# Half-channel loads of k and v, and TensorE and VectorE trading channel chunks, in a long-convolution and MLP kernel

## The chip, the cores and the metric

The kernel runs on one core of one Trainium2 chip. The metric is the device time of one execution in microseconds (us); lower is better. Every comparison uses runs of the fast state, and each kernel was timed beside runs of the kernel before on the same chip.

## The reference, cut to what matters

```python
def _A_ref(q, k, v, shift_k, ssm_k, ssm_D):          # 1 x 2048 positions x 512 channels, bf16
    k_shift = sum(k_pad[:, t:t + S, :] * shift_k[:, ks - 1 - t] for t in range(4))   # 4 taps per channel
    kv = k_shift * v
    # y = causal convolution of kv with the 2048 taps of ssm_k, by FFT of length 4096
    y = irfft(rfft(kv_pad) * rfft(kf_pad))[:S] + kv * ssm_D
    return q * y

def _B_ref(x, w1, b1, w2, b2):                        # 512 -> 1376 -> 512
    return gelu(_layernorm(x) @ w1 + b1) @ w2 + b2

x = A_q; x = x + A; x = x + B; x = x + A; x = x + B   # A is the same both times, but for its q
```

## The kernel before: the parts that matter

The kernel lists its operations, and a list scheduler with tuned priorities puts each on an engine's queue. An engine takes its queue in that order. The FFT is two stages of matmuls with tables. The 512 channels are four chunks of 128. Two chunks get their 4 taps from VectorE as elementwise operations; the other two from TensorE, which transposes k and multiplies by diagonal matrices of taps.

```python
PE_CH, PO_CH = (0, 1), ()                  # chunks of TensorE; the rest are VectorE's
LOADS = ("k", "v", 0, 1, 2, 3, 4, 5, 6, 7) # order of the transfers; 0..7 are pieces of the table S2
...
for b in range(4):                         # the long filter ssm_k, 4 blocks of 128 channels
    dma(A(0, 128, R_HRAW + b * 2048, [1, 2048]), dr(A_ssm_k, ...), 1 << 19)
...
dma(A(0, 128, R_SR, [1, 2048]), dr(A_shift_k, 0, [0, 128], [1, 2048]), 1 << 19)   # taps, 128-fold
...                                        # k: 16 positions x 512 channels in each partition
    for j in range(4):                     # a piece has 4 KB in a row
        dma(A(0, 128, R_K + 1536 + 2048 * j, [1, 2048]), dr(A_k, 2048 * j, ...), 1 << 19)
...                                        # filter: 16 transposes of 128 columns, 32 bytes apart (L740)
        src = [A(0, 128, R_HRAW + b * 2048 + a, [16, 128]) for a in range(16)]
            for a in range(16):
                r = e.transpose(QB(tl, 0, 128, a * 128, [1, 128]), src[a], IDN)
        evac(BOTH, ...)                    # PSUM to SBUF on ScalarE (L665) or VectorE (L666)
        o = A(0, 1, R_HP + b * 2048, [64, 32], [1, 4])
        tt(o, o, A(0, 1, R_D + 128 * b, ...), ALU.add, 200.0, POOL)   # adds D to the filter: 128 elements
def stage1(...):  ...   # 16 matmuls of 64 columns for a PSUM tile (L757), then an evacuation
def stage2(...):  ...   # 8 matmuls with the table S2 for a tile (L770), then an evacuation
def shift_pe(i):  ...   # 16 transposes of k (L801), 32 matmuls by tap diagonals (L813), product with v (L820)
def shift_tt(i):  ...   # 7 VectorE operations of 128x2048 for a chunk: tensor_tensor, both inputs in SBUF
```

## Time and profile before

| | before |
|---|---|
| median of 3 runs | 245.31 us (244.29 to 245.67) |
| span of the profiled run | 242.7 us |
| TensorE, VectorE, ScalarE, GpSimd busy | 229.0, 176.1, 144.7, 32.8 us |
| filter transposes (L740) | 4.80 to 10.66 us |
| VectorE's first operation on k | 17.75 us |
| first matmul of the MLP (L1045) | 86.86 us |

The first 87 us are the convolution. From 87 us on, the MLP's matmuls fill TensorE for 155.7 us. So the change has to be judged by when that first MLP matmul starts. The prediction shows the lines of this profile.

### The profile page before, as it was taken

What the parts mean: (1) busy time and instruction counts of PE and PEld (TensorE: products, weight loads), DVE (VectorE), ACT (ScalarE), POOL (GpSimd) and SP (SyncE); (2) the same over time, 40 slices, a digit from 0 to 9 for tenths busy, and PEclk for the clock granted to TensorE, in tenths of its full rate; (3) what the DMA queues carried; (4) which work ended last, traced back from release to release, by engine and by line L of the source; (5) the groups of instructions that cost most, each with busy time, mean ns of one, the idle gap of its engine ahead of it and who ended that gap; (6) DMA issues with size and microseconds to landing.
All of it is one profiled execution on the core that took longest, in us unless ns stands there. A gap on an engine that the chain in (4) does not pass through costs nothing.

```text
span 242.7 us, 5658 instructions
## 1 busy us (share of the span) xinstructions
PE 229.0 (94%) x2399; PEld 155.7 (64%) x2399; DVE 176.1 (73%) x359; ACT 144.7 (60%) x224; POOL 32.8 (14%) x71
## 2 busy tenths in 40 slices
PE   7959999786899999999999999999999999999995
PEld 3859989665899877777667665655444444444543
DVE  0459999999999998899999998797734760313022
ACT  2987899989998976755355444387004584005600
POOL 2330000000004121232131113003101010000000
PEclk9997999999999999999999999999999999999999
DMA  6999959999991000421120203302230111412012
GB/s 236 361 407 406 407 107 206 194 195 241 398 376 47 0 3 0 45 44 23 24 45 0 46 2 64 68 0 45 45 71 18 43 43 22 68 43 86 0 57 76
DMA packets 32938, 27.68 MB, mean 114 GB/s; under 512 B 17585, under 2 KB 28176, under 8 KB 32784
## 3 DMA queue, kind: packets, MB, share of 16 engines
q1 hardware_dynamic: 32766, 27.21, 40.8%
q8 instruction: 19, 0.31, 0.5%
q10 hardware_dynamic: 146, 0.10, 0.2%
q14 instruction: 7, 0.06, 0.1%
HBM read 17.34 MB, written 2.10 MB: 80 GB/s over the span
## 4 chain that ended last, share of the span: by engine, by line
PE 69%; DVE 18%; DMA 5%; ACT 3%; SPq 2%; issue 1%; POOL 1%; DVEq 0%
PE ps L1045 32%; PE ps L1078 30%; DVE ar L660 11%; DMA ar<-in_A_k_dram 5%; DVE ar L666 4%; ACT ar L665 3%; PE ps L813 2%; SPq L649 2%; PE ps L757 2%; DVE sm L970 1%; PE ps L1067 1%; DVE ar L820 1%; PE ps L801 1%; DVE ar L985 1%; POOL sm L978 1%
## 5 line engine op out<-in xcount | busy, mean ns | idle before, releaser
L1050 ACT ACTIVATE ar<-ps,sm 128x256 bf16<-128x256 f32 (+5 forms) x143 | 68.0, 521 | 73.2 <-PE ps L1045 37.9
L1045 PE MATMUL ps<-ar 128*128 128x256 bf16 (+4 forms) x572 | 82.1, 297 | 0.0
L665 ACT ACTIVATE ar<-ps 128x1024 bf16<-128x1024 f32 (+2 forms) x78 | 74.3, 1059 | 10.0 <-PE ps L757 3.8
L1078 PE MATMUL ps<-ar 128*128 128x512 bf16 (+1 forms) x341 | 79.2, 379 | 0.0
L1045 PEld LDWEIGHTS ps<-ar 128*128 128x128 bf16 (+1 forms) x572 | 53.1, 100 | 28.8 <-ACT ar L665 0.4
L660 DVE TENSOR_TENSOR ar<-ar 128x512 bf16<-128x512 bf16 (+2 forms) x104 | 63.2, 645 | 3.1 <-DMA ar<-in_A_k_dram 2.4
L1078 PEld LDWEIGHTS ps<-ar 128*128 128x128 bf16 (+1 forms) x341 | 33.2, 98 | 35.1
L1082 DVE TENSOR_TENSOR ar<-ar,ps 128x512 bf16<-128x512 bf16 x31 | 20.8, 680 | 43.7 <-PE ps L1078 43.7
L970 DVE BATCH_NORM_STATS2 sm<-ar 128x6 f32<-128x512 bf16 (+1 forms) x68 | 42.9, 649 | 0.4
L985 DVE TENSOR_SCALAR ar<-ar,sm 128x512 bf16<-128x512 bf16 x64 | 23.5, 403 | 6.3 <-POOL sm L978 6.2
L757 PE MATMUL ps<-ar 128*64 128x128 bf16 x512 | 18.9, 231 | 3.0 <-issue 1.1
L978 POOL TENSOR_TENSOR sm<-sm 128x2 f32<-128x2 f32 (+2 forms) x26 | 20.2, 778 | 2.2
L757 PEld LDWEIGHTS ps<-ar 128*64 128x64 bf16 x512 | 16.3, 117 | 5.0 <-ACT ar L665 1.9
L666 DVE CAST ar<-ps 128x1024 bf16<-128x1024 f32 (+1 forms) x17 | 19.2, 1151 | 0.3 <-PE ps L770 0.2
L976 POOL TENSOR_SCALAR sm<-sm 128x2 f32<-128x2 f32 (+2 forms) x26 | 5.3, 205 | 101.7 <-DVE sm L972 101.4
L882 PE MATMUL ps<-ar 128*128 128x128 bf16 x256 | 15.1, 220 | 1.2 <-DVE ar L660 0.7
L882 PEld LDWEIGHTS ps<-ar 128*128 128x128 bf16 x256 | 14.6, 114 | 1.6 <-DVE ar L660 0.8
L858 PE MATMUL ps<-ar 128*128 128x64 bf16 x256 | 9.2, 193 | 2.8 <-ACT ar L665 2.3
L666 DVE COPY ar<-ps 128x2048 bf16<-128x2048 bf16 (+1 forms) x5 | 4.5, 904 | 9.6 <-PE ps L740 9.5
L972 DVE BATCH_NORM_AGGREGATE sm<-sm 128x2 f32<-128x6 f32 (+1 forms) x64 | 10.2, 173 | 0.5
L858 PEld LDWEIGHTS ps<-ar 128*128 128x128 bf16 x256 | 8.1, 98 | 3.8 <-ACT ar L665 2.9
L770 PE MATMUL ps<-ar 128*128 128x128 bf16 x128 | 8.2, 220 | 0.5 <-ACT ar L665 0.5
(30 smaller groups left out, 76.9 us busy)
## 6 DMA issues: line engine op xcount, KB each, us to landing
ar<-tab_s SPq DMA_DIRECT2D x8, 512.0 KB, 15.9
ar<-ar SPq DMA_DIRECT2D x16, 256.0 KB, 6.9
ar<-in_A_ssm_k_dram SPq DMA_DIRECT2D x4, 512.0 KB, 5.5
ar<-in_A_k_dram SPq DMA_DIRECT2D x4, 512.0 KB, 10.3
ar<-in_A_v_dram SPq DMA_DIRECT2D x4, 512.0 KB, 13.8
ar<-in_A_q_dram SPq DMA_DIRECT2D x4, 512.0 KB, 13.4
out_dram<-ar SPq DMA_DIRECT2D x7, 256.0 KB, 2.0
ar<-in_B_w_dram SPq DMA_DIRECT2D x1, 1376.0 KB, 12.0
```

What stands on the lines that cost most here:

```text
L660: return P.op(eng, lambda e: e.tensor_tensor(o, a, b, op), dur, reads=[a, b] + list(more), writes=[o])
L665: return e.activation(dst, src(), AF.Copy)
L666: return e.tensor_copy(dst, src())
L757: r = e.matmul(Q(tl, 64 * ri, 64, i * 128, [1, 128]), w, m, start=True, stop=True)
L882: r = e.matmul(Q(tl, 0, 128, i * 128, [1, 128]), w, m, start=q == 0, stop=q == 1)
L970: P.op(DVE, lambda e, sj=sj, x=x: e.bn_stats(sj, x), 40.0 + 1.1 * w, reads=[x], writes=[sj], gate=gate)
L978: P.op(POOL, lambda e: e.tensor_tensor(r, v, hf, ALU.pow), 430.0 + 150.0 * n, reads=[v, hf], writes=[r])
L985: P.op(DVE, lambda e: e.tensor_scalar(o, x, m, r, ALU.subtract, ALU.mult), 335.0, reads=[x, m, r], writes=[o])
L1045: r = e.matmul(Q(tl, 0, rows, 0, [1, w]), a, m, start=dk == 0, stop=dk == 3)
L1050: P.op(ACT, lambda e, dst=dst, tl=tl, rows=rows, bias=bias, w=w: e.activation(dst, Q(tl, 0, rows, 0, [1, w]), AF.Gelu_apprx_tanh, bias=bia ...
L1078: r = e.matmul(Q(tl, 0, 128, 0, [1, 512]), ins[fc][0], ins[fc][1], start=fc == 0, stop=fc == 10)
L1082: P.op(DVE, lambda e, x=x, tl=tl: e.tensor_tensor(x, x, Q(tl, 0, 128, 0, [1, 512]), ALU.add), 640.0, reads=[x], writes=[x], tile=tl)
```

## The change: intent and diff

The intent: VectorE waits for k, so let its chunks come first and alone. Each load of k and v takes half of the channels, so a row is 256 elements or 512 bytes. VectorE gets chunks 0 and 1, which lie in the first half, and TensorE gets chunks 2 and 3. The 128-fold tap transfer is replaced by a small one and two matmuls, the filter is loaded and transposed in halves, and all priorities are tuned anew.

```diff
-PE_CH, PO_CH = (0, 1), ()
-LOADS = ("k", "v", 0, 1, 2, 3, 4, 5, 6, 7)
+PE_CH, PO_CH = (2, 3), ()
+LOADS = ("k0", "k1", "v0", "v1") + tuple(range(16))
...
-        dma(A(0, 128, R_HRAW + b * 2048, [1, 2048]), ...)
+        for c in (0, 1024):
+            dma(A(0, 128, R_HRAW + b * 2048 + c, [1, 1024]), ...)
-    dma(A(0, 128, R_SR, [1, 2048]), dr(A_shift_k, 0, [0, 128], [1, 2048]), 1 << 19)
+    dma(A(0, 1, R_SR, [1, 2048]), dr(A_shift_k, 0, [0, 1], [1, 2048]), 4096, eng=ACT)
...
-            for j in range(4):
-                dma(A(0, 128, R_K + 1536 + 2048 * j, [1, 2048]), ...)
+            for a in (0, 8):      # half of the channels, 8 rows of 512 bytes in each partition
+                dma(A(0, 128, o + 512 * a + c, [512, 8], [1, 256]), ...)
...
-        tt(o, a, A(0, 128, R_SR + 512 * c, [1, 4], [4, 128]), ALU.mult, 1200.0, POOL)
+        # two matmuls by ones spread the taps; 8 GpSimd operations of 128x128 make the diagonals
...
-        src = [A(0, 128, R_HRAW + b * 2048 + a, [16, 128]) for a in range(16)]
+        for p in (0, 64):
+            src = [A(0, 128, R_HRAW + b * 2048 + a + 16 * p, [16, 64]) for a in range(16)]
...
-                r = e.transpose(QB(tl, 0, 128, a * 128, [1, 128]), src[a], IDN)
+                    r = e.transpose(QB(tl, p, 64, a * 128, [1, 128]), src[a], IDN)
...
-        tt(o, o, A(0, 1, R_D + 128 * b, [4, 32], [1, 4]), ALU.add, 200.0, POOL)
+        tt(o, o, A(0, 1, R_D + 128 * b, [4, 32], [1, 4]), ALU.add, {DVE: 130.0, POOL: 450.0}, (DVE, POOL))
```

The tables of priorities are cut. By line, the filter's transposes are L740 before and L754 after, stage 1 is L757 and L771, stage 2 is L770 and L784, the transposes of k are L801 and L815, their diagonal matmuls L813 and L827, the product with v L820 and L834, and the MLP's first matmul L1045 and L1059. In experiments these shift by a few lines.

## The prediction

> **What bounds the kernel now.** I first read the chain that ended last, then a table of stretches, then the timelines of VectorE and ScalarE around the stretch that the change touches, then the DMA view.
>
> The chain (start, length, what) begins with transfers:
>
> ```profile
> 5.91 11.82 DMA ar<-in_A_k_dram
> 17.82 1.15 PE ps L801 x16
> 18.98 3.83 PE ps L757 x40
> ...
> 86.86 1.90 PE ps L1045 x32
> ```
>
> Up to 17.73 us the end is set by the arrival of k. To 28.6 us the chain runs over TensorE, to 86 us over VectorE with some ScalarE, and from 86.9 us to the end over the matmuls of the MLP. The stretches say the same (length, then busy us of each engine, TensorE clock, DMA share, GB/s):
>
> ```profile
> 0.00:9.00 9.00, 7.24 (x60) 4.46 (x62) 0.02 (x1) 4.20 (x3) 2.23 (x10) 1.00 0.75 291
> 9.00:15.30 6.30, 5.79 (x166) 5.29 (x164) 5.82 (x5) 6.26 (x8) 3.61 (x5) 1.00 1.03 362
> 15.30:17.75 2.45, 0.47 (x10) 0.31 (x10) 0.02 (x1) 2.23 (x3) 0.00 (x0) 1.00 1.03 411
> 17.75:22.10 4.35, 4.28 (x78) 4.11 (x80) 4.34 (x4) 2.08 (x3) 0.00 (x0) 0.61 1.03 410
> 22.10:28.60 6.50, 6.50 (x134) 6.19 (x129) 6.43 (x7) 5.57 (x5) 0.00 (x0) 1.00 1.02 405
> 28.60:87.00 58.40, 51.53 (x1028) 46.86 (x1026) 57.40 (x82) 55.39 (x60) 5.46 (x14) 1.00 0.80 195
> 87.00:242.70 155.70, 153.20 (x943) 88.47 (x940) 102.09 (x264) 68.96 (x145) 21.51 (x42) 1.00 0.17 38
> ```
>
> From 28.6 to 87 us VectorE (57.40 of 58.40) and ScalarE (55.39) are both nearly full: that stretch is a pile of work for two engines, mostly evacuations that either can take, and it ends as much earlier as both are fed earlier. After 87 us TensorE is full (153.20 of 155.70), and the change touches nothing there but the order. So what can be won lies ahead of 28.6 us, where the engines starve:
>
> ```profile
> 17.75 2.36 DVE L660 TENSOR_TENSOR ar<-ar 128x2048 bf16<-128x2048 bf16 x2 [2.44 <-DMA ar<-in_A_k_dram]
> ...
> 20.02 4.78 ACT L665 ACTIVATE ar<-ps 128x1024 bf16<-128x1024 f32 x5 [2.32 <-PE ps L757]
> 25.38 2.87 ACT L665 ACTIVATE ar<-ps 128x1024 bf16<-128x1024 f32 x2 [0.58 <-PE ps L757]
> ```
>
> VectorE waits 2.44 us for k. TensorE does only 0.47 us of work in 15.30 to 17.75: its next instruction in order is the transpose of k (L801), and the filter transform's matmuls (L757) stand behind it although their data is there. ScalarE then starves for 2.32 us on those L757. The idle TensorE also loses its clock: 0.61 on average in 17.75 to 22.10.
>
> **What the Trainium skill says.** "DMA: Bandwidth & Descriptors", section Specifications, gives 512 B as the least transfer for line rate; its section "Why small descriptors are slow (HBM only)" gives each packet a fixed overhead of some 3 cycles, so 512 B is legal but not free. The trace agrees with the second more than with the first. In its DMA records the 381 packets of 512 B of the halo loads took 27 ns each at the median, those of 1024 B 48, of 2048 B 87 and of 4096 B 162; on 16 engines that is 303, 341, 377 and 405 GB/s. The stretch with the halo in it was no better:
>
> ```profile
> DMA packets 479, 0.42 MB, mean 300 GB/s; under 512 B 45, under 2 KB 424, under 8 KB 479
> ```
>
> This is 9.2 to 10.6 us; taking out 0.225 MB of larger packets at 405 leaves 0.195 MB in 0.84 us, 231 GB/s. I take 231 to 303 for 512-byte rows.
>
> The same page ("Anatomy of one DMA — SWDGE (gpsimd) path") gives a DMA some 2 us of fixed cost, mostly the receipt of the last write. These loads are issued by SyncE, another path, but the trace has the same size: ahead of and in k are 0.10 (tables) + 2.10 (filter) + 0.52 (shift taps) + 0.20 (halo) + 2.10 (k) = 5.02 MB; by the stretches 2.62 + 2.28 + 1.00 = 5.90 MB had moved by 17.73 us. The surplus of 0.88 MB at 411 GB/s is 2.1 us from last byte to release.
>
> "TensorE: Matmul & The Clock Gate", Part 1, lets the clock fall to half after an idle window of some 3.4 us and stay there for a window. The trace agrees in kind: after the gap at 15.1 to 17.8 us (0.75 us busy in 15 to 18) the clock was 0.50 for 3.41 us, which cost TensorE about 1.7 us on the chain.
>
> "VectorE: DVE Perf Modes", section "The perf-mode tier table", gives a bf16 tensor_tensor of 2048 elements 1224 ns; the trace has 1225 (x32). It depends on the dtype and the unit step inside a row, which the change keeps, so the filter work on VectorE doesn't change: two chunks of seven such operations in both kernels.
>
> **The change, part by part.**
>
> *Half-channel loads.* VectorE's chunks are now 0 and 1, and these are all in k0, with 1 MB instead of the 2 MB of k before them. TensorE's chunks 2 and 3 come with k1. In the old kernel the last byte of k came at 17.73 - 2.1 = 15.6 us. From that: less the 128-fold broadcast of the shift taps (0.52 MB at 408 GB/s, -1.3 us), less the old k (-5.1 us), plus the filter in 2 KB rows (1024 packets x 87 ns / 16 = 5.57 us against 512 x 162 / 16 = 5.18, +0.4 us) gives 9.6 us at the end of the halo. k0 is 2048 packets x 27 / 16 = 3.5 us, or 4.5 us at 231 GB/s: last byte at 13.1 to 14.1, released at 15.2 to 16.2 us. VectorE had finished its other work at 15.3. So 1.5 to 2.4 us of its 2.44 us go. SyncE's issue is no limit: eight filter loads, two halo loads and two of k0 at about 0.45 us each end at about 6 us.
>
> *Behind it.* Last bytes of k1 at 16.6 to 18.6, v0 20 to 23, v1 23.5 to 27.7, each plus 2.1 to be usable. Chunk 0 needs v after seven operations, 8.6 us past 15.3, so at 23.9: v0 is there at 22 to 25, and chunk 1's taps can run meanwhile. The multiply of TensorE's chunks ran at 27.09 in the old kernel, v1 is there at 25.6 to 29.8. The first 256 KB of the table S2 land at 26.3 to 30.5; its first use was at 27.96. All tight, none clearly late.
>
> *TensorE order.* With k1 later than the old k and the transposes retuned behind the filter's matmuls, the gap of 15.1 to 17.8 should close, and with it the half clock. ScalarE then gets its 2.32 us back, and part of the 0.58.
>
> *Taps.* Removed: two ScalarE copies of 128x512 at 687 ns (1.37 us) and the broadcast. Added: two ones-matmuls of 512 columns (6 warm-up matmuls instead of 8 make room) and two ScalarE evacuations of 128x512 at 592 ns (the row of that shape), 1.18 us. Net -0.2 us, before the filter arrives, so nothing.
>
> *Diagonals.* GpSimd did two operations at 1178 ns; now eight 128x128 ones, by my estimate 0.3 to 0.6 us each (its 128x512 memset took 0.52), 2.4 to 4.8 us. They are needed only once k1 is in, at 19 us or later: off the path. The small add of D, 4 x 0.42 us on GpSimd, may go to VectorE, so it isn't stuck behind them.
>
> *Filter in halves.* 64 transposes of 128 columns (1.22 us per 16) become 128 of 64; L757, of the latter form, takes 0.64 us per 16, so 1.28 per block: neutral. The first half block lands some 0.6 us before a whole one; the evacuation still waits for the whole block. I give it 0.3 us.
>
> *Sum.* VectorE gains about 2.1, ScalarE about 2.3; as they share the pile, its start moves by 2.2. Plus 0.3 from the start, less 0.2 for the late v and S2: -2.3 us on the 87 us, and the MLP's 155.7 us stay. Retuning of priorities has been done for the new kernel and should give a little more: -0.3 us. 245.3 - 2.6 = 242.7 us.
>
> **The rivals.**
> 1. *The later transfers take the place of k.* The 4.2 MB of k and v take 13.8 to 18.2 us instead of 10.3, so S2 comes 2 to 6 us later (the saved broadcast taken off). For it: DMA is full to 31 us (shares of 1.02). Against it: the h2 matmuls that read S2 waited for evacuations, not for a DMA. If it holds, the first S2 at 30.5 delays TensorE and ScalarE by 2 to 3 us and the gain is gone: 245 to 246.
> 2. *TensorE bounds the stretch up to 28.6 us.* It is busy 10.78 of 10.85 us there. If its gap stays (the transposes of k1 head the line again, now until 19 us), ScalarE gains nothing and only VectorE moves: about 244. Against it: the order was retuned.
> 3. *More than the gap.* VectorE is idle to 8.98 us and ScalarE to 6.08. If the new order gives VectorE the first filter evacuations (1.23 us against 1.88 on ScalarE), another 1 to 2 us go, and with the 1.7 us of clock the time nears 240.5.
>
> **Range and chances.** The gain is capped by the starvation, about 5 us on either engine counted generously; over 2% (under 240.4) would need all of it. A loss over 2% would need S2 to be 5 us late on top of losing the gain. So 8 in 10 between 240.5 and 245.0; faster by over 2% 0.11, within 2% 0.86, slower 0.03.
>
> **What would show it.** Right: VectorE's first filter operation at 15 to 16.3 us with an idle time under 1 us before it; TensorE's clock at 1.00 in 17 to 22; no ScalarE gap over 1 us between 15 and 28; the MLP's first L1045 at about 84.3 instead of 86.9, and a last stretch still near 156 us. The 512-byte packets near 27 ns. Wrong: waits on v or the S2 table among VectorE's or TensorE's longest, a DMA rate near 230 GB/s between 9 and 25 us, or the first L1045 earlier by 2.5 while the end isn't.

## The result, and the profile after

The changed kernel took 258.54 us (median of 4 runs, 256.97 to 258.9), the kernel before 244.8 us in the same rounds. The ratio is 1.0545, 95% interval 1.0487 to 1.0603: slower. A ratio here is the mean time of one kernel's fast runs over that of the other's of the same rounds, so it is not quite the ratio of the medians quoted.

| | before | after |
|---|---|---|
| span of the profiled run | 242.7 us | 257.1 us |
| filter transposes | 4.80 to 10.66 | 5.11 to 18.97 us |
| VectorE's first operation on k | 17.75 | about 20.3 us |
| first matmul of the MLP | 86.86 | 101.21 us |
| from there to the end | 155.8 | 155.9 us |
| GpSimd busy | 32.8 | 47.3 us |

All the loss is in the convolution. This is its chain of work that ended last (start, length, what):

```profile
5.11 8.13 PE ps L754 x80
...
14.17 4.81 PE ps L754 x47
19.01 1.24 DVE ar L666
...
20.32 12.82 POOL ar L660
...
33.27 1.06 PE ps L771 x16
...
101.21 0.89 PE ps L1059 x16
```

Before, the chain began with the transfer of k. Now no transfer of k is in it. It runs over the filter's transposes up to 19 us, and then over one GpSimd operation of 12.8 us. The same two stretches in the table (length, busy us of TensorE, weight loads, VectorE, ScalarE, GpSimd, then TensorE clock, DMA share, GB/s):

```profile
5.10:19.00 13.90, 13.89 (x171) 13.89 (x173) 4.25 (x5) 2.97 (x4) 5.01 (x9) 1.00 1.15 294
...
24.90:33.30 8.40, 0.04 (x4) 0.06 (x3) 7.95 (x7) 2.85 (x3) 8.23 (x1) 0.77 1.04 380
```

In the first, TensorE is full while VectorE and ScalarE starve. Before, the same 13.9 us held 242 matmuls instead of 171, 7.10 us of VectorE and 11.41 of ScalarE. In the second, TensorE does nothing for 8.4 us while VectorE and one GpSimd operation run. The groups of instructions by shape say what the transposes cost, before and then after (count, then busy us and mean ns of one):

```profile
L740 PE MATMUL ps<-ar 128*128 128x128 bf16 x64 | 4.9, 230 | 0.5 <-DMA ar<-in_A_ssm_k_dram 0.4
L740 PEld LDWEIGHTS ps<-ar 128*128 128x128 bf16 x64 | 4.4, 150 | 1.6 <-DMA ar<-in_A_ssm_k_dram 1.5
```

```profile
L754 PE MATMUL ps<-ar 128*64 128x128 bf16 x128 | 13.3, 299 | 0.1
L754 PEld LDWEIGHTS ps<-ar 128*64 128x64 bf16 x128 | 13.0, 217 | 1.0 <-DMA ar<-tab_small 1.0
```

There are twice as many, and loading half the columns takes longer than loading all of them: 217 ns against 150. Busy time goes from 4.9 to 13.3 us. Then the timelines of GpSimd, VectorE and TensorE around 20 us:

```profile
20.32 12.81 POOL L660 TENSOR_TENSOR ar<-ar 1x128 bf16<-1x128 bf16 x1 [6.72 <-DVE ar L666]
20.15 12.69 DVE L660 TENSOR_TENSOR ar<-ar 1x128 bf16<-1x128 bf16 x12
33.27 1.06 PE L771 MATMUL ps<-ar 128*64 128x128 bf16 x16 [8.36 <-POOL ar L660]
```

GpSimd's operation is the add of D to one block of the filter, 128 elements. Three of its four instances went to VectorE (0.2 to 0.36 us). The fourth lasts just as long as VectorE's unbroken run of twelve, a small add and eleven filter operations, all with both inputs in SBUF (a group shows the shape of its first). TensorE's next stage-1 matmuls read that block, and everything behind them in TensorE's queue stands.

### The profile page after: what moved, and what is told of

It is laid out like the page before. It is cut to its first block, busy times and chain, and to the rows that moved or that the text cites. A ratio compares the mean times of both kernels' runs of the same rounds, so it can differ in the third digit from the quotient of the medians.

```text
span 257.1 us, 5820 instructions
## 1 busy us (share of the span) xinstructions
PE 237.6 (92%) x2463; PEld 165.2 (64%) x2463; DVE 177.3 (69%) x362; ACT 142.0 (55%) x224; POOL 47.3 (18%) x76
## 4 chain that ended last, share of the span: by engine, by line
PE 78%; ACT 9%; POOL 5%; DVE 3%; issue 2%; DMA 1%; ACTq 0%; DVEq 0%
PE ps L1059 30%; PE ps L1092 29%; ACT ar L665 9%; PE ps L896 5%; PE ps L754 5%; POOL ar L660 5%; PE ps L952 3%; PE ps L827 3%; DVE ar L660 2%; PE ps L771 2%; DMA ar<-tab_small 1%; PE ps L1081 1%; PE ps L872 1%; DVE ar L666 0%; PE ps L1046 0%
## 5 line engine op out<-in xcount | busy, mean ns | idle before, releaser
L1064 ACT ACTIVATE ar<-ps,sm 128x256 bf16<-128x256 f32 (+4 forms) x143 | 67.8, 521 | 67.6 <-PE ps L1059 48.8
L665 ACT ACTIVATE ar<-ps 128x1024 bf16<-128x1024 f32 (+3 forms) x80 | 73.3, 1027 | 27.3 <-PE ps L771 22.0
L1059 PE MATMUL ps<-ar 128*128 128x256 bf16 (+4 forms) x572 | 82.6, 297 | 0.0
L1059 PEld LDWEIGHTS ps<-ar 128*128 128x128 bf16 (+1 forms) x572 | 53.3, 100 | 28.1 <-ACT ar L1064 0.6
L660 DVE TENSOR_TENSOR ar<-ar 128x512 bf16<-128x512 bf16 (+3 forms) x107 | 63.7, 632 | 1.6 <-ACT ar L665 1.3
L771 PE MATMUL ps<-ar 128*64 128x128 bf16 x512 | 18.4, 224 | 9.7 <-POOL ar L660 8.4
L771 PEld LDWEIGHTS ps<-ar 128*64 128x64 bf16 x512 | 15.9, 111 | 11.4 <-issue 8.5
L992 POOL TENSOR_TENSOR sm<-sm 128x2 f32<-128x2 f32 (+2 forms) x26 | 20.3, 781 | 2.2
L666 DVE CAST ar<-ps 128x1024 bf16<-128x1024 f32 (+1 forms) x15 | 16.9, 1145 | 1.6 <-PE ps L771 0.5
L666 DVE COPY ar<-ps 128x2048 bf16<-128x2048 bf16 (+1 forms) x7 | 7.0, 995 | 14.9 <-PE ps L754 14.7
L896 PE MATMUL ps<-ar 128*128 128x128 bf16 x256 | 15.0, 220 | 1.2 <-DVE ar L660 0.6
L896 PEld LDWEIGHTS ps<-ar 128*128 128x128 bf16 x256 | 14.5, 114 | 1.5 <-ACT ar L665 0.8
L660 POOL TENSOR_TENSOR ar<-ar 1x128 bf16<-1x128 bf16 x1 | 12.8, 12807 | 6.7 <-DVE ar L666 6.7
L754 PEld LDWEIGHTS ps<-ar 128*64 128x64 bf16 x128 | 13.0, 217 | 1.0 <-DMA ar<-tab_small 1.0
L754 PE MATMUL ps<-ar 128*64 128x128 bf16 x128 | 13.3, 299 | 0.1
## 6 DMA issues: line engine op xcount, KB each, us to landing
ar<-in_B_w_dram SPq DMA_DIRECT2D x1, 1376.0 KB, 13.3
```

The costliest lines, as they stand in the source:

```text
L660: return P.op(eng, lambda e: e.tensor_tensor(o, a, b, op), dur, reads=[a, b] + list(more), writes=[o])
L665: return e.activation(dst, src(), AF.Copy)
L666: return e.tensor_copy(dst, src())
L754: r = e.transpose(QB(tl, p, 64, a * 128, [1, 128]), src[a], IDN)
L771: r = e.matmul(Q(tl, 64 * ri, 64, i * 128, [1, 128]), w, m, start=True, stop=True)
L896: r = e.matmul(Q(tl, 0, 128, i * 128, [1, 128]), w, m, start=q == 0, stop=q == 1)
```

## The experiments

The theories at the start were these. S: the transposes of half width are slow by themselves, above all because their 64 columns lie 32 bytes apart. L: VectorE's run keeps GpSimd out of SBUF. The rival of S, called T: the order is to blame, all transposes into one half of the array first, then all into the other. The rival of L: GpSimd is slow on this operation. "SBUF — State Buffer" of the Trainium skill, section "Who interferes with whom", supports L: "A DVE instruction with two SBUF inputs contends with a GpSimd instruction that reads SBUF, not with one that only writes it".

**e1, the add on VectorE alone.** Every other queue keeps its order.

```diff
-        tt(o, o, ..., ALU.add, {DVE: 130.0, POOL: 450.0}, (DVE, POOL))
+        tt(o, o, ..., ALU.add, 130.0, DVE)
```

> The changed kernel with the one change that the small add of D is allowed on VectorE only; the order of every other instruction stays. Theory L (the GpSimd add of 128 elements is held for 12.8 us because VectorE runs two-SBUF-input operations back to back, and TensorE stands behind it for 8.4 us): TensorE's gap at 24.9 to 33.3 us falls under 1.5 us, time 249 to 252. Rival W (the gap is really a wait for something else that ends at 33 us, such as k1, v or the table): the gap stays over 5 us, time over 256.

Measured: 251.25 us, ratio to the kernel before 1.0282 (1.0246 to 1.0318). TensorE's gap is gone; that stage-1 group starts at 25.28 instead of 33.27 us:

```profile
25.28 0.64 PE L771 MATMUL ps<-ar 128*64 128x128 bf16 x16 [0.20 <-ACT ar L665]
```

The stuck add is worth 7.3 us of the 13.7.

**e2, whole transposes alone**, the add left as changed.

```diff
-            src = [A(0, 128, R_HRAW + b * 2048 + a + 16 * p, [16, 64]) for a in range(16)]
+            src = [(a, A(0, 128, R_HRAW + b * 2048 + a, [16, 128])) for a in range(p // 8, p // 8 + 8)]
```

> The changed kernel with whole 128-column transposes of the filter again, eight in each of the two groups; order unchanged, add still free to go to GpSimd. Theory H (a 64-column strided weight load costs as much as or more than one of 128 columns, so the halves doubled or tripled the work): the transposes take about 5 us instead of 13.3, the filter is evacuated by 12 us instead of 20. If the GpSimd add is then done before VectorE's filter operations start it takes under 1 us and the second loss goes too: time 241 to 245. If the add is still held by VectorE: about 250. Rival (transposes are limited by the arrival of the filter's 2 KB rows): they still end at 17 us or later, time over 256.

Measured: 247.43 us, above the 241 to 245 expected, ratio 1.0119 (1.0082 to 1.0157). The timelines of GpSimd and VectorE:

```profile
14.00 0.41 POOL L660 TENSOR_TENSOR ar<-ar 1x128 bf16<-1x128 bf16 x1 [0.53 <-DVE ar L666]
15.11 12.58 DVE L660 TENSOR_TENSOR ar<-ar 128x2048 bf16<-128x2048 bf16 x11 [1.07 <-DMA ar<-in_A_k_dram]
```

The same add on the same engine now takes 0.41 us, because it comes 1.1 us before VectorE's run. So GpSimd is not slow here, and the two losses are coupled: only the late transposes pushed the add into VectorE's run. VectorE's first operation on k is at 15.11 us, where the prediction had it.

**e3, both undone** (the edits of e1 and e2 together).

> Both of the above: add on VectorE, whole transposes; what is left of the change are the half-channel loads, the exchange of the chunks, the taps by matmul and the new order. If the two losses are all, 241 to 244, and the predicted gain of the loads shows at last. If the loads with 512-byte rows cost something themselves (table S2 or v late): 246 to 250, with a wait for a DMA among the longest of TensorE or VectorE.

Measured: 247.34 us, ratio 1.0132 (1.0085 to 1.0178), the same as e2. Some 3 us to the kernel before remain. They get their own experiments below.

**e4, the two halves in turn.** The 64-column transposes stay, but the left and the right half of each follow one another.

```diff
-            src = [A(0, 128, R_HRAW + b * 2048 + a + 16 * p, [16, 64]) for a in range(16)]
+            src = [(a, q, A(0, 128, R_HRAW + b * 2048 + a + 16 * q, [16, 64])) for a in range(p // 8, p // 8 + 8) for q in (0, 64)]
```

> The changed kernel, half transposes kept with the same strided weights, but alternating between the two column halves of the array (as the filter transform's matmuls of the same size do) instead of 16 in a row on one half. Theory S (the stride of 32 bytes in the weight load[...] is the cost): still about 1.6 us per 16, 13 us in all, time 256 to 260. Theory T (consecutive loads into the same half can't overlap, alternation does): about 0.7 us per 16, 5.5 us in all, time as in the run with whole transposes.

Measured: 255.28 us at the median of four runs, one of them slow; the ratio, 1.0416 (1.0363 to 1.0469), is of the three fast ones. Neither theory's time came. The group of transposes:

```profile
L754 PE MATMUL ps<-ar 128*64 128x128 bf16 x128 | 8.3, 285 | 0.9 <-issue 0.8
L754 PEld LDWEIGHTS ps<-ar 128*64 128x64 bf16 x128 | 8.0, 217 | 1.6 <-issue 0.9 <-DMA ar<-in_A_ssm_k_dram 0.7
```

One weight load still takes 217 ns, but the group takes 8.3 us instead of 13.3, so with the halves in turn the loads overlap more: the 128 records sum to 27.8 us, and cover 8.0 us here, 13.0 in the changed kernel. Neither S nor T stood as it was put: a single load is no shorter, and the order decides how much of it shows. The add still lasts 12.80 us, from 16.03 us on.

**e7, a probe of the lock** (e3 and two operations that nothing needs; a single look): once the first half of k is in, GpSimd writes 128 elements, then adds 128.

```diff
+    P.op(POOL, lambda e: e.memset(pr, 0.0), 150.0, reads=[kk], writes=[pr])
+    tt(pr, kk, pr, ALU.add, 450.0, POOL)
```

> As e3_both_undone, with two probes on GpSimd that nothing waits for, released when k1 has landed (19 us), in the middle of VectorE's run of filter operations (15.4 to 28 us): a memset of 128 elements on one partition, which only writes SBUF, then an add of 128 elements that reads two SBUF operands. Theory L (GpSimd's reads wait for VectorE's two-input operations): memset under 0.3 us, the add until about 28 us, 7 to 9 us. Rival (the long add of the changed kernel had another reason): add about 0.4 us. Time as in e3, within 1%.

Measured: 246.98 us, and on GpSimd's timeline:

```profile
17.91 0.20 POOL L765 MEMSET ar<- 1x128 bf16 x1 [5.36 <-DMA ar<-in_A_k_dram]
18.20 9.58 POOL L660 TENSOR_TENSOR ar<-ar 1x128 bf16<-1x128 bf16 x1
```

In the midst of VectorE's run the write goes through at once, and the operation that reads lasts until 27.78 us. VectorE's run ends at 27.49. L holds. The operation did not get through between two of VectorE's instructions: it took the rest of the run, not the rest of one instruction of 1.1 us. In the changed kernel TensorE, which waits for the add, confirms its end: it starts 0.14 us after it.

**e8, half transposes alone in the kernel before.**

```diff
-        src = [A(0, 128, R_HRAW + b * 2048 + a, [16, 128]) for a in range(16)]
+        src = [(p, a, A(0, 128, R_HRAW + b * 2048 + a + 16 * p, [16, 64])) for p in (0, 64) for a in range(16)]
```

> The kernel before with half transposes alone, 16 in a row on each half of the array; the order of all else is the same. Theory H: the transposes take about 13 us instead of 4.9 and end near 18 us; the evacuations behind them start late, and 4 to 8 us come through to the end: 248 to 253. Rival (in the kernel before VectorE and TensorE wait for k until 17.7 anyway, so the start is hidden): 244 to 246.

Measured: 249.33 us, ratio 1.0197 (1.0167 to 1.0227). Here too the weight loads take 216 ns and the transposes 13.3 us. The loss does not need the rest of the change.

**e12, contiguous columns** (a wrong result on purpose; the kernel of e1, a single look).

```diff
-            src = [A(0, 128, R_HRAW + b * 2048 + a + 16 * p, [16, 64]) for a in range(16)]
+            src = [A(0, 128, R_HRAW + b * 2048 + 64 * a + 16 * p, [1, 64]) for a in range(16)]
```

> Gives a wrong result on purpose: as e1_add_vector (halves, 16 in a row on one half of the array, add on VectorE), but each half transpose takes 64 neighbouring columns of the filter instead of every sixteenth. Theory S (the 32-byte stride in a 64-column weight load is the cost): 16 transposes take 0.6 to 0.9 us instead of 1.6, weight load mean falls from 217 to about 110 ns, all 128 in 5 to 7 us, time 244 to 248. Theory T (staying on one half of the array is the cost): 1.5 us and more per 16 as before, time 250 to 252.

Measured: 246.71 us against e1's 251.25, and in the group of transposes:

```profile
L754 PE MATMUL ps<-ar 128*64 128x128 bf16 x128 | 8.4, 253 | 0.2 <-DMA ar<-tab_small 0.2
L754 PEld LDWEIGHTS ps<-ar 128*64 128x64 bf16 x128 | 8.1, 133 | 1.2 <-DMA ar<-tab_small 1.1
```

S had asked for some 110 ns and 5 to 7 us, so it holds in part. With 16 in a row on one half, the step of 32 bytes makes 4.9 of the 8.4 us more of transposes (13.3 less 4.9). The other 3.5 us are mostly the order and not the doubled count: stage 1's matmuls (L771) have this shape and contiguous columns too, but their halves alternate, and they take 0.64 us per 16, so 5.1 for 128. Mending either the order (e4) or the step (e12) leaves 8.3 to 8.4 us; no run made transposes with both mended. Why a strided load of 64 columns is slower than one of 128 is not shown by any run. The Trainium skill names a candidate in "TensorE: Matmul & The Clock Gate", section "Weight-path perf modes — Fast Weight Load (FWL) and DoubleRow": fast weight load "is on when the number of weights is 128". The 150 and 217 ns fit that, but no run here shows the mode.

**e5, k and v in whole rows** (e3 and 4 KB rows). The theory here was R: the 512-byte rows make the last 3 us.

```diff
-                dma(A(0, 128, o + 512 * a + c, [512, 8], [1, 256]), ...)
+                dma(A(0, 128, o + a + c, [1, 2048]), ...)          # c = 4096 * half, a in (0, 2048)
```

> As e3_both_undone, with k and v loaded again in 4 KB rows of all four chunks (two loads in place of each half), in the same places of the queue; only the loads differ, but VectorE's filter now waits for all of k. Theory R (the 512-byte rows move at about 290 GB/s and make k1, v and the table S2 late, which costs more than k0 wins): the DMA rate between 9 and 20 us rises from about 290 to over 380 GB/s, VectorE's first filter operation comes 1 to 2 us later than in e3 (at 16.5 to 17.5), the first matmul on S2 comes before 30 us instead of at 32.2, time 243.5 to 246. Rival O (what is left is the new order, whatever the loads): time 247 to 249, since only the later start of VectorE is added.

Measured: 247.97 us, ratio 1.0137 (1.0101 to 1.0173), no better than e3, although the DMA queues moved 397 GB/s in 10 to 20 us instead of 283. As the whole of the remainder, R falls.

**e6, only v in whole rows** (e3 with the edit of e5 for v).

> As e3_both_undone, but only v in 4 KB rows; k0 and k1 stay halves with 512-byte rows. Theory R: v and S2 come about 2 us earlier, the first matmul on S2 at about 30 us, VectorE's start stays at 15.4, time 245 to 246.8. If it is k1 for the transposes of TensorE's chunks that decides, not S2: no change, 247 to 248.

Measured: 247.24 us, ratio 1.011 (1.0071 to 1.0149), as e3. The timelines of TensorE and ScalarE show a new suspect:

```profile
19.73 1.86 PE L815 MATMUL ps<-ar 128*128 128x128 bf16 x16 [2.82 <-DMA ar<-in_A_k_dram]
21.63 9.21 ACT L665 ACTIVATE ar<-ps 128x2048 bf16<-128x2048 bf16 x9 [2.66 <-PE ps L815]
```

TensorE's chunks are in the second half of k, usable at 19.7 us. Its transposes of k head its queue, and stage-1 matmuls whose data has long been there stand behind them. ScalarE, which evacuates those, starves. I call this theory Q. Before, the same wait ended at 17.8 us.

**e9, the half loads alone in the kernel before**, every queue in its old order.

```diff
-            for j in range(4):
-                dma(A(0, 128, R_K + 1536 + 2048 * j, [1, 2048]), ...)
+            for c, a in ((256, 0), (256, 8), (0, 0), (0, 8)):
+                dma(A(0, 128, R_K + 1536 + 512 * a + c, [512, 8], [1, 256]), ...)
```

> The kernel before, all of its order kept on the four compute engines, with k and v loaded as the change does: channel halves in 512-byte rows, the half of VectorE's chunks (here 2 and 3) first. It isolates the loads. My prediction's step (VectorE's filter starts earlier and the pile moves with it): first filter operation at 16.0 to 16.6 us instead of 17.75, time 242 to 244. Theory Q (TensorE's transposes of the other half stand in its queue before the filter transform's matmuls, and that half now comes later than the old k, at 19.5 to 20.5 us): VectorE starts earlier but TensorE's gap grows by about 2 us, time 245 to 247.

Measured: 247.64 us, ratio 1.0121 (1.0092 to 1.0150). TensorE, ScalarE and VectorE:

```profile
20.25 1.87 PE L801 MATMUL ps<-ar 128*128 128x128 bf16 x16 [2.82 <-DMA ar<-in_A_k_dram]
23.15 2.85 ACT L665 ACTIVATE ar<-ps 128x1024 bf16<-128x1024 f32 x3 [4.66 <-PE ps L757]
22.15 1.23 DVE L666 COPY ar<-ps 128x2048 bf16<-128x2048 bf16 x1 [4.14 <-PE ps L801]
```

VectorE began at 15.66 instead of 17.75, and the MLP at 90.44 instead of 86.86. The half that comes second costs more than VectorE wins by the half that comes first; VectorE itself then stands 4.14 us for the transposes. The whole k landed at 17.73 us before, the second half at 20.16 here. The rate, 282 instead of 392 GB/s in 10 to 20 us, accounts for some 2 us of that (an estimate: 2.1 MB of k at the one and at the other), so it is the short rows more than the split.

**e10, the new taps alone in the kernel before** (whole loads, the added operations put in; the old order was meant).

```diff
-    dma(A(0, 128, R_SR, [1, 2048]), dr(A_shift_k, 0, [0, 128], [1, 2048]), 1 << 19)
+    dma(A(0, 1, R_SR, [1, 2048]), dr(A_shift_k, 0, [0, 1], [1, 2048]), 4096, eng=ACT)   # and the taps by matmul
```

> The kernel before with the change's taps alone: one row of shift taps spread by two ones-matmuls, diagonals by eight GpSimd operations, add of D on VectorE, whole loads in 4 KB rows, old order otherwise. The broadcast of 0.52 MB ahead of k is gone, so k should land 1.3 us earlier, at about 16.4 us, for TensorE and VectorE alike: 242.8 to 244 against 244.4. Rival (the start is then bound by the filter transform, not by k): within 0.3% of the kernel before.

Measured: 244.63 us, ratio 1.0004 (0.9981 to 1.0027). k is there 1.5 us earlier, and TensorE's clock stays at 1.00, yet the MLP starts at 86.78 us, within 0.1 us of before. ScalarE again waits 3.09 us behind the transposes of k. But TensorE's order was not the old one: in its queue the first transposes of k stand behind 112 stage-1 matmuls, before behind 160, so three tiles further forward. The wait is in part of the edit's own making, and e14 is the cleaner look at the taps alone.

**e11, e10 and k in halves.**

> As e10_taps_old_order, with k alone in channel halves of 512-byte rows, VectorE's half first. Prediction's step: VectorE at about 15 us, 1.4 us ahead of e10, time 0.5 to 1.5 us under e10. Theory Q: the half for TensorE lands at 18 to 19 us, later than the whole k of e10 by about 2 us, time 0.5 to 2 us over e10.

Measured: 248.51 us, ratio 1.0143 (1.0107 to 1.0178). The transposes wait until 18.30 us for the second half (3.13 us), and ScalarE is idle for 4.66 us behind them. TensorE's order is e10's. VectorE began at 16.67 us, no earlier than in e10 (16.29): the first half of k landed at 15.27, but its evacuations kept it, so the expected start at about 15 us missed.

The next four test Q itself: they only put off the first transposes of k, behind three or four more tiles of stage 1. A line in the scheduler does it, as in e13 and e16 (in e14 and e15 the value is 18000):

```diff
+    P.HOLD = {**P.HOLD, late[0]: 20000.0}      # late[0]: the first group of k transposes
```

**e13, e9 with later transposes.**

> The kernel of e9 (the kernel before with half-channel loads of k and v), with the TensorE half's first transposes issued 48 filter-transform matmuls (three tiles) later. Theory Q (the in-order TensorE queue stands behind a late half of k): the 2.8 us wait at 20.25 and ScalarE's 4.66 us of idle time shrink to under 1.5 us each, the MLP's first matmul comes 1.5 to 3 us earlier than e9's 90.44, time 245 to 246. Rival (the filter's own loads and the VectorE queue of 12 operations set the end): waits move, time stays at 247.2 to 248.

Measured: 251.8 us, ratio 1.0287 (1.025 to 1.0325), outside both expectations. The edit reshuffled more than it was meant to: VectorE now stood 3.43 us for the transposes' evacuation, and TensorE 3.22 us for S2, which its queue now reached early. It says nothing on Q, except that order is worth 4 us here.

**e14, e10 with later transposes** (behind 176 stage-1 matmuls, one tile behind the old place), all other queues as they were.

> The kernel of e10 (the kernel before with the taps by matmul, whole loads), with the first transposes 64 filter-transform matmuls (four tiles) later and every other queue in the same order. Theory Q: ScalarE's idle 3.09 us before 18.01 falls under 1 us, everything behind it comes 1 to 2.5 us earlier, time 242 to 243.6, so faster than the kernel before by up to 1%. Rival (VectorE's 12 operations in a row set the end of this stretch whatever TensorE does): 244.3 to 244.9, as e10.

Measured: 243.96 us, ratio 0.9984 (0.9946 to 1.0022). ScalarE's wait fell from 3.09 to 0.42 us, as Q had it, but another of 1.26 us came at 24.9 us, and no gain is told apart from zero. It has the lowest median of all versions, and still is not shown to beat the kernel before.

**e15, e11 with later transposes**, all other queues as they were.

> The kernel of e11 (taps by matmul and k in halves), with the same four tiles moved ahead of the first transposes, every other queue in the same order. Theory Q: ScalarE's 4.66 us of idle time falls under 1.5 us and the time from 248.5 to 244.5 to 246. If the late half of k costs in itself, not through the order, 247.5 to 248.5.

Measured: 246.04 us, ratio 1.0049 (0.9991 to 1.0107), against e11's 1.0143. ScalarE's wait fell from 4.66 to 0.84 us; its lines in e11 and then in e15:

```profile
19.96 10.19 ACT L665 ACTIVATE ar<-ps 128x1024 bf16<-128x1024 f32 x10 [4.66 <-PE ps L777]
18.39 5.76 ACT L665 ACTIVATE ar<-ps 128x1024 bf16<-128x1024 f32 x6 [0.84 <-PE ps L777]
```

Q holds in this kernel: one group of 16 transposes in the wrong place of one queue was worth some 2.3 us by the ratios, though the two intervals just touch, and three of the four tiles make up for e10's own displacement. In the same order, k in halves (e15) ended 2.1 us after k whole (e14) by the medians; the intervals of the ratios overlap.

**e16, e3 with later transposes.**

> The changed kernel with whole-row transposes of the filter and the add on VectorE (e3), with its k transposes 48 filter-transform matmuls later. Theory Q: the 2.04 us wait for k and ScalarE's 1.87 us go, time 245.3 to 246.3. Rival (the tables of stage 2, which land at 32.2 in e3, set the end there): the wait at 32.2 grows by what is won and the time stays at 246.9 to 247.6.

Measured: 247.08 us, ratio 1.0117 (1.0082 to 1.0152): the rival's number. ScalarE and TensorE show why:

```profile
13.31 14.71 ACT L665 ACTIVATE ar<-ps 128x1024 bf16<-128x1024 f32 x15 [0.97 <-PE ps L771]
30.82 1.50 PE L784 MATMUL ps<-ar 128*128 128x128 bf16 x24 [2.47 <-DMA ar<-tab_s]
31.47 2.85 ACT L665 ACTIVATE ar<-ps 128x1024 bf16<-128x1024 f32 x3 [3.45 <-PE ps L784]
```

ScalarE's run is now unbroken up to 28 us, and what was won is lost at once to S2, the table of stage 2, which is queued behind v and is usable only at 30.8 us. What is waited for is not its first piece: by the profile the wait ends with the fifth of sixteen, landed at 30.69 us, while the first four had landed at 26.93 to 29.09. So stage 2's tuned order seems to ask for a later piece first, and to start with an earlier one is a remedy that no run tried.

**e18, e16 with v in whole rows**: this and nothing else, so that S2 comes earlier.

> e16 with v in whole rows, k still in halves; all queues of the compute engines are the same. Theory: in e16 the stage-2 tables, queued behind v's 512-byte rows, land at 30.8 and set the start of stage 2 (2.47 us of TensorE, 3.45 of ScalarE); v in whole rows frees the queue about 2 us earlier (2.1 MB at 283 against 392 GB/s), stage 2 starts at 28.5 to 29.3 and the time is 245.0 to 246.2. Rival (something behind it, like VectorE's run, catches the gain): 246.7 to 247.4 as e16.

Measured: 245.51 us, ratio 1.0039 (1.0013 to 1.0064). TensorE and ScalarE:

```profile
29.36 1.50 PE L784 MATMUL ps<-ar 128*128 128x128 bf16 x24
30.01 2.86 ACT L665 ACTIVATE ar<-ps 128x1024 bf16<-128x1024 f32 x3 [0.82 <-PE ps L784]
```

The wait for S2 is gone; the DMA queues moved 374 GB/s in 20 to 28 us instead of 289. These are two waits in a row: undoing the first alone (e16) gave 0.3 us, the second alone (e6) 0.1 us, both 1.8 us.

**e17, e5 with an earlier product from PSUM.** e5 had S2 early too. There I blamed PSUM tiles that VectorE's run holds.

```diff
-            P.op(DVE, g, 1135.0, reads=[v], writes=[o], tile=tl)
+            P.op(DVE, g, 1135.0, reads=[v], writes=[o], tile=tl, prio=3e9 if i == 0 else 0.0)
```

> The kernel of e5 (the changed kernel, both losses undone, k and v in whole rows), with VectorE's first product from PSUM moved ahead of the last four of its run of filter operations; TensorE's and ScalarE's queues are the same. Theory: in e5 the run of 12 held two PSUM tiles, so stage 2 stood 2.54 us at 30.8; with one tile free early that wait falls under 0.8 us and the time goes from 247.97 to 245.5 to 246.7. Rival (VectorE's sum of work sets the end of this stretch, whatever its order): 247.4 to 248.3.

Measured: 247.88 us, ratio 1.015 (1.0131 to 1.0169): my theory missed, and the rival's number came. VectorE and TensorE:

```profile
17.26 8.16 DVE L660 TENSOR_TENSOR ar<-ar 128x2048 bf16<-128x2048 bf16 x8 [3.58 <-DMA ar<-in_A_k_dram]
...
32.28 1.51 PE L784 MATMUL ps<-ar 128*128 128x128 bf16 x24 [1.49 <-DVE ar L837]
```

The wait at 30.8 became one of 1.91 us at 26.6 and one of 1.49 at 32.3. From 17.26 to 37.9 us the chain lies on VectorE. In this order VectorE's sum of work is the limit, and with whole rows it starts at 17.26 instead of 15.52 us (e18). That fits that k in halves is worth something once the rest is in order, but e17 and e18 also differ in other points, and e14 and e15 point the other way.

## Why the prediction was wrong

The prediction gave 242.7 us and a range to 245.0; the kernel took 258.54. By its own steps:

1. *Half-channel loads bring VectorE's start forward by 1.5 to 2.4 us.* Right in itself: 15.11 us in e2, 15.66 in e9, against the predicted 15 to 16.3. The rate of the 512-byte rows, predicted as 231 to 303 GB/s, was 283 to 293 while k and v alone moved (13 to 25 us); their packets took 32 to 34 ns at the median of a run, not 27. In the changed kernel the early start did not show, as VectorE's queue stood behind late evacuations until 20.2 us.
2. *"Filter in halves: neutral."* This step failed first. The working took the price of a 64-column transpose from L757 (0.64 us for 16), whose weight columns are contiguous and whose loads alternate between the halves of the array; the new transposes have columns 32 bytes apart, and go to one half 16 in a row. Four blocks cost 13.3 us instead of the 5.1 that 1.28 each makes. Without the stride (e12), or with the halves in turn (e4), they cost 8.3 to 8.4. Alone in the kernel before (e8) this makes 5.0 us of end time.
3. *"The small add of D may go to VectorE, so it isn't stuck behind" the diagonals.* One of four stayed on GpSimd and was stuck, but behind VectorE: 12.8 us, of which 8.4 stopped TensorE, worth 7.3 us of end time (e1). No rival had it. Had step 2 been right, it would not have happened (e2).
4. *"TensorE order: the gap should close."* Argued from the fact of retuning, not from a line. The prediction's second rival had the mechanism right: without the losses of steps 2 and 3, the transposes of k stand at the head of the queue until 18.3 to 20.3 us and ScalarE starves (e6, e9, and e11, whose order is in part to blame); put off, the gap closes (e15). But its "about 244" had VectorE's gain in it, and e9 shows a loss of 3 us with that gain there.
5. *"All tight, none clearly late" for S2.* The first rival was right here: once TensorE is early enough, S2 comes late behind 512-byte rows (e16, 2.47 us), and with v in whole rows the wait goes (e18). The landing was as predicted (first 256 KB at 26.9 us in e16, predicted 26.3 to 30.5); wrong was which piece is needed first, as the wait was for the fifth. Its size, 245 to 246 us, had none of the other losses in it.
6. *Taps and diagonals off the path.* Right as far as seen: e10 is 1.0004 times the kernel before, though k came 1.5 us earlier. The eight diagonals took 5.5 us, above the estimate of 2.4 to 4.8, but ended at 13.6 us, well before k was transposed.
7. *The sum took 1 us of an earlier start as 1 us of an earlier end.* e9 shows otherwise: with every compute queue in its old order, VectorE began 2.1 us earlier, later stood 4.14 us for TensorE, and the end came 3 us later. With k 1.5 us earlier e10 ended unchanged, but in a changed order; e14, with VectorE 1.0 us earlier, shows no gain clear of noise, and its interval leaves room for 1.3 us. In this stretch three engines and the DMA queue take turns, and in each queue the next wait was only 1 to 3 us off.
8. *The MLP's stretch stays.* Right: 155.8 and 155.9 us.

Along one path of undoing, the medians (of different rounds, so good to some tenths) give 7.3 us for the stuck add (258.54 to e1), 3.9 for the half transposes (e1 to e3), and 1.8 for TensorE's order and the late table together (e3 to e18). What is left, 1.2 us from e18 to the kernel before of its rounds (244.3), was not traced. Also open are e14's second wait and what a full retuning of the priorities for e18 would give.

## What to carry to other kernels

Take the price of a new instruction from a row with the same access pattern and the same order among its neighbours, not just the same shape: here a stride in the weight columns, and 16 in a row on one half of the array, turned "neutral" into 8 us. A tiny operation on GpSimd that reads SBUF belongs ahead of a run of two-input VectorE operations, or on VectorE itself, because it may wait for the whole run (12.8 us here). And when a transfer is split so that one engine's half comes first, look at who needs the other half, at what stands behind that one's wait in its in-order queue, and at whether shorter rows make that half later than the whole was (20.2 instead of 17.7 us in e9).

## What the Trainium skill lacked or had wrong

- "SBUF — State Buffer", "Who interferes with whom", says how long the shared ports are held ("for the whole instruction") only of VectorE's perf modes; of two-input operations it says only that they contend. Here an add on GpSimd waited out a run of twelve back-to-back VectorE instructions: it took 12.81 us for 128 elements, and 9.58 us in e7, where a GpSimd write in the same run took 0.20 us. That reads are blocked and writes are not is as the page says.
- "TensorE: Matmul & The Clock Gate", "LDWEIGHTS (loading the stationary operand)", gives a time that depends on the count of columns alone. In the records 64 columns 32 bytes apart took 217 ns each, contiguous ones 133, and 128 columns 32 bytes apart 150. Nor does the time of a row of loads follow from that count: with the halves in turn, the same 217 ns loads and their matmuls took 8.3 us for 128 instead of 13.3 (e4).
- "DMA: Bandwidth & Descriptors", "Specifications", names 512 B as enough for line rate. In 13 to 25 us, with 512-byte rows of k and v the queues moved 283 to 293 GB/s (after, e2, e3, e9), with 4 KB rows 398 (e5) and 407 (before).
